# Three partial writes at the end of a kernel: waits between them removed, row numbers found on GpSimd

## The chip, the core and the metric

The kernel runs on one core of one Trainium2 chip. The metric is the time of one execution on the device, in microseconds (us). Within the core, TensorE (PE in the profile; PEld is its weight load) multiplies matrices, VectorE (DVE) and ScalarE (ACT) work elementwise, GpSimd (POOL) does small elementwise work and issues the indirect DMAs, and SyncE (SP) issues the other DMAs. A name with q (POOLq) is that engine's instruction sequencer.

## The reference

An attention block with normalized queries and keys, and behind it a mixture-of-depths block: of each batch's 448 tokens the 128 with the highest score go through two layers, and their rows of the output are replaced.

```python
# attention: batch 8, heads 12, seq 448, head_dim 64
q_n, k_n = rmsnorm(q, g_q), rmsnorm(k, g_k)
attn = softmax(scale * q_n @ k_n.T)           # over the keys
x = (attn @ v).transpose(0, 2, 1, 3).reshape(8, 448, 768)
# mixture of depths: D 768, F 1024, capacity 128
scores = np.einsum('bsd,d->bs', x, w_gate)
out = x.copy()
for b in range(B):
    top_idx = np.argpartition(-scores[b], capacity)[:capacity]
    xe = x[b, top_idx]
    h = np.maximum(xe @ w1, 0.0)
    ye = h @ w2
    g = 1.0 / (1.0 + np.exp(-scores[b, top_idx]))
    out[b, top_idx] = x[b, top_idx] + g[:, None] * ye
```

## The kernel before

`fast` holds the whole computation for the shapes at hand; `general` is compiled beside it, behind a branch (line 1436), and does not run here. The order of work is written out by hand: the loop at the end of `fast` goes through steps, in each of which it emits attention work, and one piece of the two layers' work of an earlier batch; `mixture` is a generator that is advanced one piece at a time.

Attention is tiled by groups of four heads. When a batch's attention is done, the whole batch x is stored to the output in DRAM (`store_x`, line 455, on SyncE's queue). Its scores are ranked, and `select` (line 539, GpSimd) writes the 128 selected rows by indirect DMA into a small DRAM buffer, from which they are loaded into `xe`, a tile of 128 partitions by 770 columns: 768 of the row, column `DM` (768) with the gate g, and column `DM + 1` with the row's number in the output.

`mixture` then computes the two layers for a group of batches. Batches 1 to 6 go in pairs; batch 0 and batch 7, the last, go alone. It transposes `xe` (line 610), finds the row numbers (line 622, VectorE), multiplies by w1 (line 639) and by w2 (line 659 or 683). `gated` (line 596, VectorE) multiplies a result in PSUM by the gate and adds it to `xe`; `write` (line 587, GpSimd) sends columns of `xe` by indirect DMA to those rows of the output that the tile `row` names.

For all batches but the last, one write sends whole rows of 768 columns. For the last, `parts_out` (line 583) cuts the columns into three parts, which are computed and written one after the other: columns 0 to 384, 512 to 768, and 384 to 512. Each write views the output as rows of the part's width, so each part needs its own row numbers: the number times 2, 3 or 6, plus 0, 2 or 3. `row` has one column for each part, and all three are computed by VectorE in one place, ahead of the layers.

The framework puts in the waits between engines and DMAs from the tiles and tensors that instructions read and write. All writes go to the tensor `out`, so each write of line 587 waits until the one before it has landed. `select` already lifts such waits for its four writes with `declare_no_dep`, as they go to different rows. In the build the last batch's second write waits for the first write's DMA and VectorE; the third waits for the second write's DMA, for an earlier DMA that used the same semaphore, and for VectorE.

Of the kernel before, what the change touches and what calls it, by code (L numbers as in the profile page):

```python
# [13 lines left out]
OP = mybir.AluOpType  # L14
# [54 lines left out]
def fast(  # L69
# [21 lines left out]
    nc = tc.nc  # L91
# [9 lines left out]
    DM = H * D  # L101
# [57 lines left out]
    for jj in range(NJ // 2):  # L159
# [4 lines left out]
        out=gg, in0=loads.gcol[:, 0:1], scalar=scale, in1=loads.gcol[:, 1:2], op0=OP.mult, op1=OP.mult  # L164
# [399 lines left out]
    def mixture(g):  # L564

        n, bs = CAP, groups[g]
        G = len(bs)
        wide = 128 * G
        xe = [xes.pop(b) for b in bs]
# [4 lines left out]
        def bank():  # L574

            if PER * now[0] >= units:
                return ps_sc.tile([128, 512], F32, tag="sc", name="sc")
            return ps_moe.tile([128, 512], F32, tag="moe", name="moe_ps")

        half = NDC // 2  # L580
        rows = []

        parts_out = ((0, HD), (DM - 2 * HD // 3, DM), (HD, DM - 2 * HD // 3)) if last else ((0, DM),)

        def write(i, k):
            c0, c1 = parts_out[k]
            nc.gpsimd.indirect_dma_start(  # L587
                out=out.flatten_outer_dims().rearrange("r (k c) -> (r k) c", c=c1 - c0),
                out_offset=bass.IndirectOffsetOnAxis(ap=rows[i][:n, k : k + 1], axis=0),
                in_=xe[i][:n, c0:c1],  # L590
                in_offset=None,
            )

        def gated(i, cols, ps):
            x = xe[i]
            nc.vector.scalar_tensor_tensor(  # L596
                out=x[:n, cols],
                in0=ps[:n, : cols.stop - cols.start],
                scalar=x[:n, DM : DM + 1],
                in1=x[:n, cols],  # L600
                op0=OP.mult,
                op1=OP.add,
            )

        for i, x in enumerate(xe):
            for a in range(2):
                ps = ps_sc.tile([128, 512], F32, tag="sc", name="xeT_ps") if a else bank()
                for d in range(half):
                    dc = half * a + d
                    nc.tensor.transpose(  # L610
                        out=ps[:, 128 * d : 128 * d + n],
                        in_=x[:n, 128 * dc : 128 * (dc + 1)],
                        identity=ident[:n, :n],
                    )
                nc.scalar.copy(  # L615
                    out=xeT[:, half * a : half * (a + 1), i, :n],
                    in_=ps[:, : half * 128].rearrange("p (i t) -> p i t", t=128)[:, :, :n],
                )
                if a == 1:
                    row = moe_pool.tile([128, len(parts_out)], I32, name="row", bufs=4)  # L620
                    for k, (c0, c1) in enumerate(parts_out):
                        nc.vector.tensor_scalar(
                            out=row[:n, k : k + 1],
                            in0=x[:n, DM + 1 : DM + 2],
                            scalar1=float(DM // (c1 - c0)),
                            scalar2=float(c0 // (c1 - c0)),
                            op0=OP.mult,
                            op1=OP.add,
                        )
                    rows.append(row)  # L630
                if a == 1 or G == 1:
                    yield

        chunks = 4 // G
        for f0 in range(0, NFC, chunks):
            ps = bank().rearrange("p (i g t) -> p i g t", g=G, t=128)
            for i in range(chunks):
                for dc in range(NDC):
                    nc.tensor.matmul(  # L639
                        out=ps[:, i, :, :n],  # L640
# [8 lines left out]
                out=hT[:, f0 : f0 + chunks, 0:G, :n], in_=ps[:, :, :, :n], func=AF.Relu  # L649
# [3 lines left out]
        if G == 1:  # L653
            for k, (c0, c1) in enumerate(parts_out if last else ((0, HD), (HD, DM))):
                ps = bank()
                h = c0 // HD
                for fc in range(NFC):
                    w = w2.get((fc // HF, h), ring.get("B12"))
                    nc.tensor.matmul(
                        out=ps[:n, : c1 - c0],  # L660
                        lhsT=hT[:, fc, 0, :n],
                        rhs=w[:, fc % HF, c0 - HD * h : c1 - HD * h],
                        start=(fc == 0),
                        stop=(fc == NFC - 1),
                    )
                    if fc == NFC // 2 - 1:
                        yield
                gated(0, slice(c0, c1), ps)
                if last or h:
                    write(0, k if last else 0)  # L670
                yield
            return
# [28 lines left out]
        for first in (0, 1) if PER * now[0] < units else (1, 0):  # L701
# [8 lines left out]
            if done_both:  # L710
                nc.vector.tensor_tensor(
                    out=s4[:, :, :n], in0=a12[:, :, :n], in1=s2[:, :, :n], op=OP.subtract
# [13 lines left out]
        product(ps, s4, w2[1, 1])  # L726
        gated(0, high, ps)
        write(0, 0)
        yield
        product(main, s3, ring[3], first=False)  # L730
# [7 lines left out]
        product(main, a22, ring[0], first=False)  # L738
        gated(1, low, main)
        write(1, 0)  # L740
        if g < len(groups) - 2:
            reload(1)
# [164 lines left out]
    def piece(q):  # L907

        nonlocal moe, done
        if half == 1 and single(q):  # L910
            return False
        pieces[0] += 1
        if next(moe, moe) is not moe:
            return True
        if ready.get(done, q + 1) > q:
            return False
        moe = mixture(done)
        pieces[:] = 1, 10 if len(groups[done]) == 1 else 17
        done += 1
        next(moe)  # L920
        return True
# [6 lines left out]
    while done < len(groups) or tasks:  # L928
        now[:] = q, 0
        k = PER * q  # L930
# [558 lines left out]
```

## Time and profile before

| | us |
|---|---|
| median of 3 runs | 518.45 (517.85 to 519.04) |
| the profiled execution | 513.42 |
| its span | 511.7 |
| PE busy in the span | 491.6 (96%) |
| DVE busy | 354.0 (69%) |
| ACT busy | 274.8 (54%) |
| POOL busy | 187.0 (37%) |

The profile is of one execution. The span runs from its first to its last instruction; what lies around it (1.7 us) belongs to the execution's time. Lines of the timeline give start, duration, engine, line, operation, tiles (out<-in), shapes, and in brackets the idle time before it on its engine and what ended that. A wait for several semaphores is put down to the one that came last.

### The profile page before, as it was taken

How to read it: one execution, taken by the hardware profiler on the slowest of the kernel's cores; microseconds unless marked ns; L12 is line 12 of the kernel's file. 1: busy time of each engine (PE TensorE's matmuls, PEld its weight loads, DVE VectorE, ACT ScalarE, POOL GpSimd, SP SyncE). 2: the span in 40 equal slices, each digit the busy share in tenths (PEclk: the TensorE clock that was granted, in tenths of full speed). 3: DMA queues.
4: the chain of work that ended last, by engine and by line, in shares of the span. 5: the costliest groups of instructions: out<-in, count | busy, mean ns of one | idle time of the engine just before them, and what ended most of it. 6: DMA issues, size and time to landing. Idle time of an engine off the chain costs nothing. (4 is left out here: it accounts for less than half of the span.)

```text
span 511.7 us, 11121 instructions
## 1 busy us (share of the span) xinstructions
PE 491.6 (96%) x4429; PEld 279.4 (55%) x4429; DVE 354.0 (69%) x670; ACT 274.8 (54%) x507; POOL 187.0 (37%) x104
## 2 busy tenths in 40 slices
PE   5999999988999999999999999999999899999994
PEld 4544445435555444666654454665554454786683
DVE  4566898699866898996687886777567686623201
ACT  4787886866757466665454737654634536310000
POOL 4694548444524174427123085036220022020102
PEclk9999999999999999999999999999999999999998
DMA  8977889999964673899461989567423318232601
GB/s 294 387 247 257 271 272 365 326 296 319 283 204 129 214 248 121 283 323 331 134 201 26 350 280 302 190 191 207 136 72 88 110 38 260 89 109 58 221 3 36
DMA packets 49295, 105.82 MB, mean 207 GB/s; under 512 B 11571, under 2 KB 26420, under 8 KB 49234
## 3 DMA queue, kind: packets, MB, share of 16 engines
q1 hardware_dynamic: 45826, 98.70, 59.9%
q0 software_dynamic: 3264, 6.31, 3.7%
q8 instruction: 37, 0.61, 0.5%
q14 instruction: 24, 0.20, 0.1%
q10 hardware_dynamic: 144, 0.00, 0.0%
HBM read 84.37 MB, written 28.50 MB: 221 GB/s over the span
## 5 line engine op out<-in xcount | busy, mean ns | idle before, releaser
L337 ACT ACTIVATE p<-sc,rinv 128x448 f32<-128x448 f32 x336 | 186.0, 641 | 88.3 <-PE sc L328 74.3
L256 POOL TENSOR_TENSOR rinv<-ss,neg_half 128x14 f32<-128x14 f32 (+1 forms) x49 | 135.7, 2775 | 184.4 <-DVE ss L255 164.9
L328 PE MATMUL sc<-qT,kT 64*64 64x448 f32 x1344 | 152.7, 545 | 1.0 <-DVE qT L307 0.8
L352 PE MATMUL av<-p,v 64*64 64x448 f32 x1344 | 147.0, 537 | 0.0
L368 DVE TENSOR_TENSOR sum<-sum,p 128x896 f32<-128x896 f32 x107 | 116.5, 1089 | 8.1 <-ACT p L337 1.9
L352 PEld LDWEIGHTS av<-p,v 64*64 64x64 f32 x1344 | 57.6, 133 | 69.6 <-issue 62.3
L328 PEld LDWEIGHTS sc<-qT,kT 64*64 64x64 f32 x1344 | 52.5, 132 | 69.3 <-issue 43.8
L255 DVE TENSOR_REDUCE ss<-sq 128x14 f32<-128x910 f32 (+1 forms) x49 | 52.1, 1074 | 11.9 <-ACT sq L246 11.6
L639 PE MATMUL moe_ps<-xeT,w 128*128 128x256 f32 (+1 forms) x288 | 56.1, 347 | 0.0
L539 POOL DMA_INDIRECT selected<-x,rank x32 | 35.8, 1118 | 47.7 <-DVE x L531 39.7
L639 PEld LDWEIGHTS moe_ps<-xeT,w 128*128 128x128 f32 x288 | 46.2, 191 | 6.8 <-issue 2.6
L246 ACT ACTIVATE sq<-tok 128x896 f32<-128x896 f32 (+1 forms) x49 | 45.9, 949 | 5.9 <-DMA tok<-in_tok_dram 5.6
L443 DVE TENSOR_TENSOR x<-x_ps,rden 112x512 f32<-112x512 f32 x48 | 32.5, 687 | 20.8 <-PE x_ps L441 18.3
L467 DVE SCALAR_TENSOR_TENSOR prod<-x,wg 112x256 f32<-112x256 f32 x96 | 40.6, 423 | 2.9
L587 POOL DMA_INDIRECT out_dram<-xe,row x10 | 10.5, 1052 | 85.7 <-DVE xe L596 67.9
L639 PE MATMUL sc<-xeT,w 128*128 128x256 f32 (+1 forms) x192 | 32.2, 328 | 0.3 <-ACT xeT L615 0.3
L441 PE MATMUL x_ps<-ident,xT 128*112 128x128 f32 x192 | 28.8, 276 | 2.0 <-DVE x L443 2.0
L639 PEld LDWEIGHTS sc<-xeT,w 128*128 128x128 f32 x192 | 28.8, 191 | 2.8 <-ACT xeT L615 0.5
L287 DVE SCALAR_TENSOR_TENSOR qT<-qT,gg,bc 128x896 f32<-128x896 f32 x22 | 25.3, 1149 | 4.4 <-DMA bc<-rows 4.4
L512 DVE SCALAR_TENSOR_TENSOR cmp<-score_rows,gate,earlier 112x448 f32<-112x448 f32 x32 | 21.9, 684 | 9.1 <-ACT score_rows L502 8.1
L441 PEld LDWEIGHTS x_ps<-ident,xT 128*112 128x112 f32 x192 | 21.8, 134 | 10.3 <-issue 4.5
L368 DVE TENSOR_TENSOR sum<-p 128x896 f32<-128x896 f32 x24 | 25.9, 1078 | 1.8 <-ACT p L337 1.8
(87 smaller groups left out, 331.9 us busy)
## 6 DMA issues: line engine op xcount, KB each, us to landing
tok<-in_tok_dram SPq DMA_DIRECT2D x48, 448.0 KB, 6.6
qT<-in_qT_dram SPq DMA_DIRECT2D x24, 448.0 KB, 6.6
kT<-in_kT_dram SPq DMA_DIRECT2D x24, 448.0 KB, 7.1
v<-in_vp_dram SPq DMA_DIRECT2D x24, 448.0 KB, 7.6
out_dram<-x SPq DMA_DIRECT2D x8, 1344.0 KB, 9.0
bc<-rows SPq DMA_DIRECT2D x44, 224.0 KB, 6.4
ring<-mixed SPq DMA_DIRECT2D x22, 384.0 KB, 5.3
xe<-selected SPq DMA_DIRECT2D x8, 385.0 KB, 3.7
```

The costliest lines, as they stand in the source:

```text
L246: nc.scalar.activation(out=sq[:, h, :, 0:D], in_=t[:, h], func=AF.Square, scale=scale)
L255: nc.vector.tensor_reduce(out=ss[:, h], in_=sq[:, h], axis=AX.X, op=OP.add)
L256: nc.gpsimd.tensor_tensor(out=rinv[:, h].rearrange(flat), in0=ss[:, h].rearrange(flat), in1=neg_half.to_broadcast([128, (h.stop - h.start) ...
L328: nc.tensor.matmul(out=scs[hh][D * c : D * (c + 1), 0:S], lhsT=get("kT", n)[r, c, D * i : D * (i + 1)], rhs=get("qT", n)[r, c, :], start=True,
L337: nc.scalar.activation(out=p[:, hh], in_=scs[hh][:, 0:S], func=AF.Exp, scale=rinvs[n, 1][:, hh, i : i + 1],)
L352: nc.tensor.matmul(out=avs[n][c][D * hh : D * (hh + 1), 0:S], lhsT=get("v", n)[r, hh, i, :], rhs=probs[u][r, hh], start=(i == 0), stop=(i ...
L368: nc.vector.tensor_tensor(out=sums[n], in0=probs.pop(u - 1) if begins else sums[n], in1=probs.pop(u), op=OP.add)
L441: nc.tensor.transpose(out=ps[:CP, j, :], in_=t[:, j, :], identity=ident)
L443: nc.vector.tensor_tensor(out=xs[b][:, :, col : col + 128].rearrange("p j (h d) -> p j h d", d=D), in0=ps[:CP].rearrange("p j (h d) -> p j ...
L467: nc.vector.scalar_tensor_tensor(out=prod[:, 0 : GH * D], in0=xs[b][:, j, cols], scalar=1.0, in1=wg[:, cols], op0=OP.mult, op1=OP.mult, ac ...
L539: w = nc.gpsimd.indirect_dma_start(out=t[:, :], out_offset=bass.IndirectOffsetOnAxis(ap=rank[:, j : j + 1], axis=0), in_=x[:, j, :], in_of ...
L639: nc.tensor.matmul(out=ps[:, i, :, :n], lhsT=w1[:, dc, 128 * (f0 + i) : 128 * (f0 + i + 1)], rhs=xeT[:, dc, 0:G, :n], start=(dc == 0), sto ...
```

## The change

`declare_no_dep` is called for the last batch's second and third writes, so that they do not wait for the writes before them in the same call of `mixture`. The row numbers of the first part (for the other batches the only part) are still found on VectorE, in the same place. Those of the second and third part are now found on GpSimd, each just ahead of its write.

```diff
         half = NDC // 2
-        rows = []
+        rows, written = [], []
...
+        def find_row(engine, i, k):
+            c0, c1 = parts_out[k]
+            engine.tensor_scalar(
+                out=rows[i][:n, k : k + 1],
+                in0=xe[i][:n, DM + 1 : DM + 2],
+                scalar1=float(DM // (c1 - c0)),
+                scalar2=float(c0 // (c1 - c0)),
+                op0=OP.mult,
+                op1=OP.add,
+            )
+
         def write(i, k):
             c0, c1 = parts_out[k]
-            nc.gpsimd.indirect_dma_start(
+            if k > 0:
+                find_row(nc.gpsimd, i, k)
+            w = nc.gpsimd.indirect_dma_start(
                 out=out.flatten_outer_dims().rearrange("r (k c) -> (r k) c", c=c1 - c0),
                 out_offset=bass.IndirectOffsetOnAxis(ap=rows[i][:n, k : k + 1], axis=0),
                 in_=xe[i][:n, c0:c1],
                 in_offset=None,
             )
+            for other in written if k > 0 else ():
+                tc.declare_no_dep(w.ins, other.ins, reason="other columns or other rows")
+            written.append(w)
...
                     row = moe_pool.tile([128, len(parts_out)], I32, name="row", bufs=4)
-                    for k, (c0, c1) in enumerate(parts_out):
-                        nc.vector.tensor_scalar(
-                            out=row[:n, k : k + 1],
-                            in0=x[:n, DM + 1 : DM + 2],
-                            scalar1=float(DM // (c1 - c0)),
-                            scalar2=float(c0 // (c1 - c0)),
-                            op0=OP.mult,
-                            op1=OP.add,
-                        )
                     rows.append(row)
+                    find_row(nc.vector, i, 0)
```

In the build the second write then waits for VectorE and for GpSimd's row number; the third for VectorE, for GpSimd's row number, and for the earlier DMA that used the same semaphore. The two row-number operations on GpSimd wait for nothing.

## The prediction

> **What bounds the kernel now.** I read the busy shares first, then the chain that ended last, then the timeline of the end, then the instructions and waits of line 587. Over the whole span TensorE is the bound:
>
> ```profile
> PE 491.6 (96%) x4429; PEld 279.4 (55%) x4429; DVE 354.0 (69%) x670; ACT 274.8 (54%) x507; POOL 187.0 (37%) x104
> ```
>
> Nothing on TensorE changes, so the question is the piece of the span in which TensorE is done. The chain that ended last shows it:
>
> ```profile
> 5 pieces in order of time: start us, us, what
> 504.15 0.96 DMA out_dram<-xe,row
> 505.11 2.63 issue
> 507.74 0.04 POOLq L1436
> 507.77 0.19 issue
> 507.96 0.96 POOL out_dram L587
> ```
>
> The third write starts at 507.96, 2.85 us after the second was issued, with nothing but that write's journey in between. The timeline has the three writes (L587) and the three vector operations that make their data (L596):
>
> ```profile
> 499.19 0.62 DVE L596 SCALAR_TENSOR_TENSOR xe<-sc,xe 128x384 f32<-128x384 f32 x1 [16.29 <-PE sc L659]
> 500.51 0.95 POOL L587 DMA_INDIRECT out_dram<-xe,row  x1 [16.55 <-DVE xe L596]
> 502.64 0.48 DVE L596 SCALAR_TENSOR_TENSOR xe<-sc,xe 128x256 f32<-128x256 f32 x1 [2.84 <-PE sc L659]
> 504.15 0.96 POOL L587 DMA_INDIRECT out_dram<-xe,row  x1 [2.69 <-issue]
> 504.43 0.35 DVE L596 SCALAR_TENSOR_TENSOR xe<-sc,xe 128x128 f32<-128x128 f32 x1 [1.30 <-PE sc L659]
> 507.96 0.96 POOL L587 DMA_INDIRECT out_dram<-xe,row  x1 [2.85 <-issue]
> ```
>
> Data are ready at 499.81, 503.12 and 504.78; writes begin 0.70, 1.03 and 3.18 us later. Line 587 between 500.6 and 504.2 shows what the GpSimd sequencer waited for (columns: count, min/median/max ns, first and last start):
>
> ```profile
> L587 POOL DMA_INDIRECT out_dram<-xe,row x2: 954/956/958, 500.5 to 504.1; - x2
> L587 POOLq EVENT_SEMAPHORE  x2: 17/1650/3282, 503.1 to 503.9; - x2
> DMA to landing us min/median/max: 2.6/2.8/3.0
> ```
>
> The first semaphore wait, that of the second write on the first, is over at 503.1: 500.51 plus the 2.6 us landing. The second, that of the third on the second, lasts 3.28 us, from 503.9 to 507.2: 504.15 plus 3.0. So the two waits are of quite different worth: the second write's data come at 503.12, just as the first write lands; the third write's data wait 2.4 us for a landing.
>
> At the end SyncE waits for all writes, then the engines meet and stop:
>
> ```profile
> SPq L1413 <- DMA out_dram<-xe,row: 24.2, 1, 24.2
> L1413 POOLq DRAIN  x3: 45/113/2559, 508.2 to 511.4; - x3
> L1413 DVEq DRAIN  x2: 10/26/41, 507.6 to 511.2; - x2
> ```
>
> The third write lands 2.3 us after its start, at about 510.3, and the closing takes 1.4 us to 511.7. VectorE reaches its closing DRAIN only at 507.6, PE at 505.7: these would matter if the third write landed before 507.6.
>
> **What the change leaves alone.** The built instruction lists of PE, ACT and SP are the same instruction for instruction; so is GpSimd's up to the first of these writes. Batches before the last have one part and one row-number operation, still on VectorE. The change therefore acts after 482.6 us only.
>
> **Removed: two VectorE operations** (row numbers 2 and 3; three such operations of 142 ns ran from 482.6). VectorE is idle from there to 499.19, waiting for TensorE: worth 0. That idle stretch is the cover; without it they would be worth 0.28 us at most.
>
> **Removed: the second write's wait for the first.** It ended at 503.1, the data at 503.12. Worth between 0 and, if the late wait is why that start came 1.03 instead of 0.70 us after the data, 0.33 us. I take 0, as the write now waits for two things again (VectorE and GpSimd's own row number): start 504.15, end 505.11.
>
> **Added: row number 2 on GpSimd**, issued behind the first write. GpSimd is idle from 501.46 to 504.15 and the operation waits for nothing, so it is ready before the data at 503.12 if it takes under 1.6 us. No row shows this operation on GpSimd. The nearest are small operations with an int32 side, and above them the power:
>
> ```profile
> L196 POOL CAST token_f<-token_i 112x4 f32<-112x4 int32 x1 | 0.2, 186 | 0.1
> L195 POOL IOTA token_i<- 112x4 int32 x1 | 0.1, 127 | 0.0
> L256 POOL TENSOR_TENSOR rinv<-ss,neg_half 128x7 f32<-128x7 f32 x2 | 3.0, 1491 | 1.7 <-DVE ss L255 1.7
> ```
>
> One value per partition, multiply and add: between 0.13 (IOTA) and 1.5 us (seven powers). I take 0.2, by the cast, since that is a plain conversion like this. Cost here 0.
>
> **Added: row number 3 on GpSimd**, queued behind the second write. It starts about 0.1 us after 505.11 and ends at 505.4. This one is not covered: the third write waits for it, and only for it, since the data (504.78) are older.
>
> **Removed: the third write's wait for the second.** In the build it now waits for VectorE, for GpSimd's row number, and for the earlier user of its semaphore, a write of selected rows from 454.58 that landed long ago. From the release to a write's start the trace has two prices: 0.27 us where the write stood ready (data at 476.59 and 482.72, writes at 476.86 and 483.00), and 0.78 where a semaphore wait went just before (507.18 to 507.96). Row number 3 at 505.4 gives 505.7 or 506.2. I take the middle, 505.9, since one wait (on data, 504.78) will be over early and the other not.
>
> **The sum.** The third write moves from 507.96 to 505.9: −2.06 us. It issues for 0.96 as before, lands 2.3 us after its start, at 508.2, behind VectorE's DRAIN at 507.6, so the closing still hangs on the write. Contention: the second write's 128 KB move within 505.6 to 506.8 in the trace, the third's 64 KB from about 507.4; no overlap. Span 511.7 − 2.06 = 509.64. The profiled execution took 513.42 (1.72 around its span) and would take 511.36. The median of the runs is 518.45, 5.03 above the profiled one; I carry that over: 518.45 − 2.06 = 516.4.
>
> Bounds: everything good, the second write 0.27 after its data (503.4, ends 504.35), row number 3 done at 504.65, third write 0.27 after its data: 505.05, −2.9. Everything poor, the second write 0.3 later for its extra wait, row number 0.4, start 0.78 behind that: 506.7, −1.25.
>
> **Two rules against the change.** *Row*: on GpSimd the first IOTA and the first CAST of the program follow each other at 37.99 and 38.18 with no gap, and the first two powers average 1491 ns: no cold start. *Rule*: the Trainium skill, GPSIMD Engine Reference, § 2.1, says the first call of a freshly loaded library kernel pays about 6 us for its code, which no profiled instruction shows. By the rule row number 2 would end at 507.6, the third write would start at 509.4 and the span end at 513.1: +1.4, 519.9. By the row, −2.06. [...]
>
> **Rivals.**
> *A new wait takes the old one's place.* Row number 3 stands between the two writes on GpSimd. If it costs what the power does, 1.49 us, the third write starts at 505.11 + 0.1 + 1.49 + 0.78 = 507.5: −0.5, 518.0, no change that can be told. For: software operations on GpSimd are dear here (2.8 us for 14 powers). Against: the cast.
> *Slower: cold code.* The 6 us above, paid once, at row number 2. Place: GpSimd after 501.46. Up to about 1.9 us it is hidden by the wait for data; from there it delays both writes, and beyond 1.9 + 2.06 = 4 us the kernel is slower than before: 519.9 at 6. Against: no first use in this trace shows it.
> *It does not do what it says.* If something else held the third write behind the second, say room for descriptors, nothing would be won: 518.4. Against: at 454.58, 455.82, 457.07 and 458.32 four such writes of 128 rows leave 1.25 us apart though each takes 2.4 to 3.0 us to land.
>
> **How the numbers follow.** Two kernels can be told apart here from 0.2% on, 1.04 us. The main course has 0.82 (gain 1.25 to 2.9, 515.5 to 517.2); the new wait or something holding the write 0.10 (517.5 to 518.5); cold code 0.05; an unseen loss in the closing 0.03 (about 518). Run-to-run spread is ±0.6 on the median. Of the main course nearly all is faster by over 0.2%, and a little of the second rival: faster 0.84, same 0.10, slower 0.06. The range takes the bounds and part of the spread: 515.2 to 517.7.
>
> **What would show it.** Right: the long semaphore wait of line 587 (3.28 us) gone; two small GpSimd operations, near 501.6 and 505.2, of about 0.2 us; the third write near 505.9; the second still near 504.15; GpSimd's issue to landing unchanged. Wrong: a third write after 507, a row-number operation over 1 us or a gap before it, a second write later than 504.5, or a closing over 1.4 us after the last landing.

## The result and the profile after

| | before | after |
|---|---|---|
| median, all runs side by side | 517.89 us (22 runs, 513.88 to 520.69) | 516.17 us (22 runs, 513.47 to 520.07) |
| ratio, 95% interval | | 0.9988 (0.9965 to 1.0011) |
| a second session, e1 below | 515.32 us (23 runs) | 514.76 us (12 runs), ratio 0.9991 (0.9961 to 1.0021) |
| profiled execution, span | 513.42, 511.7 us | 513.47, 511.8 us |

The medians moved by 1.7 and 0.6 us the way that was forecast (the ratio of the first two medians alone is 0.9967), but both intervals include no change at all. The runs of one kernel lie 5 to 7 us apart, several times what is looked for. They follow TensorE's granted clock: of the 22 runs of after, the one at 513.47 had 1.000 and the one at 520.07 had 0.991.

The profile has to decide, and its two spans are equal too. The timeline of after (GpSimd's writes are now L600, the gate additions L612) shows why:

```profile
501.05 0.62 DVE L612 SCALAR_TENSOR_TENSOR xe<-sc,xe 128x384 f32<-128x384 f32 x1 [16.41 <-PE sc L667]
502.37 0.95 POOL L600 DMA_INDIRECT out_dram<-xe,row  x1 [16.55 <-DVE xe L612]
503.34 0.21 POOL L587 TENSOR_SCALAR row<-xe 128x1 int32<-128x1 f32 x1
504.50 0.48 DVE L612 SCALAR_TENSOR_TENSOR xe<-sc,xe 128x256 f32<-128x256 f32 x1 [2.84 <-PE sc L667]
505.80 0.99 POOL L600 DMA_INDIRECT out_dram<-xe,row  x1 [2.24 <-DVE xe L612]
506.28 0.35 DVE L612 SCALAR_TENSOR_TENSOR xe<-sc,xe 128x128 f32<-128x128 f32 x1 [1.30 <-PE sc L667]
506.87 0.18 POOL L587 TENSOR_SCALAR row<-xe 128x1 int32<-128x1 f32 x1
507.41 1.00 POOL L600 DMA_INDIRECT out_dram<-xe,row  x1 [0.36 <-POOL row L587]
```

In this execution the first gate addition starts at 501.05, in that of before at 499.19. That is 1.86 us of drift in work that the change doesn't touch: in a second profile of the changed kernel (e1) it starts at 499.37. So times at the end are counted from that operation on, and its distance to the end of the span is called the tail. It is 12.52 us before (511.71 − 499.19) and 10.70 after (511.75 − 501.05). The third write starts at 8.77 before and at 6.36 after.

Two views confirm what released it. In the chain of after, the end of it, the long "issue" of before is gone; the data, the row number and the write follow each other:

```profile
506.28 0.36 DVE xe L612
506.65 0.03 POOLq L600
506.68 0.11 POOL out_dram L600
506.79 0.08 issue
506.87 0.18 POOL row L587
507.05 0.14 issue
507.18 0.04 POOLq L1444
507.22 0.18 issue
507.41 1.00 POOL out_dram L600
```

And the sequencer's semaphore waits for line 600 from 500 us on: the wait of 3282 ns is gone, the longest is 1043 ns, until the third part's data are there:

```profile
L600 POOLq EVENT_SEMAPHORE  x2: 17/530/1043, 505.0 to 505.6; - x2
```

### The profile page after: what moved, and what is told of

It reads as the page before. It is cut to its first block, busy times and chain, and to the rows that moved or that the text cites. A ratio compares the mean times of both kernels' runs of the same rounds, so it can differ in the third digit from the quotient of the medians.

```text
span 511.8 us, 11121 instructions
## 1 busy us (share of the span) xinstructions
PE 493.3 (96%) x4429; PEld 280.1 (55%) x4429; DVE 354.0 (69%) x668; ACT 274.8 (54%) x507; POOL 188.1 (37%) x106
## 4 chain that ended last, share of the span: by engine, by line
PE 60%; ACT 1%; DVE 1%; issue 0%; POOL 0%; POOLq 0%; ACTq 0%
PE sc L328 13%; PE av L352 13%; PE moe_ps L647 8%; PE moe_ps L691 6%; PE sc L647 6%; PE side_ps L691 5%; PE x_ps L441 2%; PE sc L667 2%; PE den_ps L396 1%; ACT p L337 1%; PE denT_ps L420 1%; PE moe_ps L667 1%; PE row_ps L496 0%; DVE xe L612 0%; PE xeT_ps L626 0%
## 5 line engine op out<-in xcount | busy, mean ns | idle before, releaser
L600 POOL DMA_INDIRECT out_dram<-xe,row x10 | 10.7, 1066 | 82.9 <-DVE xe L612 70.1
```

## The experiments

Starts and tails are in us after the first gate addition. "Landing" is from the third write's start to the moment SyncE saw it landed. Each row is one profile of its kernel; before and after have two.

| | second write | third write | landing | tail |
|---|---|---|---|---|
| before / e12 before again | 4.96 / 4.97 | 8.77 / 8.48 | 2.35 / 2.31 | 12.52 / 12.20 |
| after / e1 after again | 4.75 / 4.74 | 6.36 / 6.37 | 2.96 / 3.19 | 10.70 / 10.95 |
| e2 waits only | 4.22 | 5.87 | 3.46 | 10.73 |
| e3 third only | 4.73 | 6.37 | 2.98 | 10.74 |
| e4 rows only | 4.73 | 8.57 | 2.31 | 12.27 |
| e5 late third | 4.75 | 7.09 | 3.27 | 11.75 |
| e6 swap, before | 4.66 | 7.81 | 2.26 | 11.48 |
| e7 swap, after | 4.74 | 6.36 | 2.31 | 10.09 |
| e8 swap, waits only | 4.22 | 5.87 | 2.27 | 9.55 |
| e11 no third write | 4.75 | – | – | 9.46 |

**e1, the changed kernel again.**

> The changed kernel again, for its time beside the kernel before on one chip. The tail is counted from the start of the first of the three vector operations that add the gate (384 columns) to the end of the span: 12.52 us in the profile of before (511.71 - 499.19), 10.70 in that of after (511.75 - 501.05). Theory (the third write no longer waits for the second's landing, and the rest of the span is untouched): tail 10.3 to 10.9, third write 6.3 to 6.5 after the first vector operation (8.77 before), time 1.5 to 2.2 us shorter, ratio about 0.996 to 0.997. Rival (the gain is eaten elsewhere): same tail, but ratio 1.000 or above.

Tail 10.95, span 510.3; ratio 0.9991 (0.9961 to 1.0021). The tail agrees with the theory, nearly, and repeats. The ratio stays between the two: the expected 0.996 to 0.997 lies inside the interval, and so does 1.000.

**e12, the kernel before again**, for the spread on the other side.

> The kernel before once more, for the spread of its tail, which so far rests on one profile (12.52) and on the kernel with the row numbers moved and the waits kept (12.27). Theory (the tail of before is set by two landings one after the other): 12.1 to 12.8, the third write's wait 2.9 to 3.4 us long. Rival (12.52 was a long one, and the gain of 1.6 to 1.8 us is partly chance): 11.8 or less.

Tail 12.20, the wait 2.99 us. With two profiles on each side the gain in the tail is 12.36 − 10.83 = 1.5 us (1.25 to 1.8 by pairs).

**e2, waits lifted, row numbers left on VectorE.** A memset of a tile that nobody reads stands where the row numbers stood, so that there still is a GpSimd instruction ahead of each write.

```diff
             if k > 0:
-                find_row(nc.gpsimd, i, k)
+                nc.gpsimd.memset(moe_pool.tile([128, 1], F32, name="spacer", bufs=2), 0.0)
...
-                    find_row(nc.vector, i, 0)
+                    for k in range(len(parts_out)):
+                        find_row(nc.vector, i, k)
```

> The waits are lifted, but all three row numbers are found on VectorE as in the kernel before; ahead of the second and third write a 128x1 memset on GpSimd, of a tile that nobody reads, stands between the writes in place of the row numbers. Theory (lifting the wait is all; the row numbers on GpSimd only add a wait on GpSimd itself): second write 4.2 to 4.75 after the first vector operation (after: 4.75), third 5.6 to 6.2 (after: 6.36), tail 10.0 to 10.7, so equal to the changed kernel or up to 0.7 better. Rival (it is the row numbers on GpSimd that help, VectorE's signal being slow): tail 11.5 to 12.5.

The timeline of e2:

```profile
502.51 0.48 DVE L612 SCALAR_TENSOR_TENSOR xe<-sc,xe 128x256 f32<-128x256 f32 x1 [2.84 <-PE sc L668]
503.27 0.96 POOL L600 DMA_INDIRECT out_dram<-xe,row  x1 [1.82 <-DVE xe L612]
504.24 0.11 POOL L599 MEMSET spacer<- 128x1 f32 x1
504.30 0.35 DVE L612 SCALAR_TENSOR_TENSOR xe<-sc,xe 128x128 f32<-128x128 f32 x1 [1.30 <-PE sc L668]
504.93 0.96 POOL L600 DMA_INDIRECT out_dram<-xe,row  x1 [0.58 <-DVE xe L612]
```

With one thing to wait for, both writes start 0.28 us after their data (502.99 and 504.65), 0.5 us earlier than in after. So the rival falls: the row numbers on GpSimd don't help. In after the second write starts 0.8 us after its data, behind a separate semaphore wait; the third is then late because the second is still issuing, to 506.79, and its row number follows that. Yet the tail is 10.73, no better, and just over the expected range. The landing took 3.46 us instead of 2.3. Something else holds the end; e5 to e8 look for it. As a whole e2 has the lowest ratio here, 0.9968 (0.9935 to 1.0001), but not clearly faster than before or after.

**e3, only the third write freed; e4, only the row numbers moved.**

```diff
-            for other in written if k > 0 else ():
+            for other in written if k > 1 else ():    # e3
+            for other in ():                          # e4
```

> As the changed kernel, but only the third write's waits are lifted; the second still waits for the first to land. Theory (the second write's wait ended as its data came, and is worth 0 to 0.3): second write 4.7 to 5.1 after the first vector operation, third 6.3 to 6.8, tail 10.7 to 11.0. Rival (both waits carry the gain, as they stand in one chain): tail 11.5 or more.

> The row numbers of the second and third part on GpSimd, all waits between the writes kept. Theory: the writes start as before, 4.9 to 5.2 and 8.7 to 9.1 after the first vector operation; tail 12.4 to 12.9; the row numbers take about 0.2 us each and stand ready before their data or landings. Rival (the row numbers' place is what helps): tail under 12.

e3's tail is after's (10.74), and so is its third write's start; e4's tail is before's (12.27, a little under the expected 12.4, and its two writes start 0.1 to 0.2 us earlier than expected). The whole gain is the third write's wait; the second's was worth nothing that shows beside a row number on GpSimd. In both, the second write starts at 4.73 instead of 4.96, so these 0.23 us don't come from the lifted wait. They need no row number either: in e6 below, which has none on GpSimd, it starts at 4.66. Where they come from is open.

**e5, the third write later**, by finding its row number three times.

```diff
-                find_row(nc.gpsimd, i, k)
+                for _ in range(3 if k == 2 else 1):
+                    find_row(nc.gpsimd, i, k)
```

> The changed kernel with the third part's row number found three times over on GpSimd, so that the third write starts some 0.5 us later. What is tested: in the changed kernel and in the one with the waits lifted alone the third write starts 6.36 and 5.87 after the first vector operation, yet both tails are 10.7; in both, one of the third write's packets starts only when the 16 KB of instructions that are fetched from 6.9 to 8.3 after the first vector operation have passed. Theory (the fetch, not the write's start, now sets the end): third write at 6.8 to 7.0, tail 10.6 to 11.0. Rival (the tail follows the write's start, one for one, and the kernel with the waits alone was an accident): tail 11.2 to 11.5.

The write started at 7.09 and the tail was 11.75: neither. The end is no fixed floor, as the theory had it: 0.73 us later start, 0.8 to 1.05 us longer tail. The landing was again 3.27 us, with another fetch in the way (below). So the theory was formed anew: not one fetch at a fixed time, but any instruction fetch that overlaps the write's data delays a share of them.

The DMA view of after from 507.9 to 509.9, in slices of 0.05 us, and of 509.35 to 509.9 in slices of 0.014 us, shows the coincidence. First the long window:

```profile
GB/s 0 0 82 0 0 0 328 0 0 0 0 0 0 164 0 0 0 0 0 0 0 492 246 328 164 0 0 0 0 0 82 0 0 0 0 0 0 0 0 0
q8 instruction: 1, 0.02, 3.8%
```

then the short one:

```profile
GB/s 0 0 0 0 0 298 0 0 0 0 0 0 0 0 0 0 0 0 0 0 0 0 0 0 0 0 0 0 0 0 0 0 0 0 0 0 0 0 0 0
q0 software_dynamic: 2, 0.00, 4.9%
```

The value 328 at 508.2 is the 16 KB instruction packet; 3.8% of 16 engines over 2 us is 1.22 us, so it ends at 509.42. Of the third write's 16 packets of 4 KB, 15 start from 508.98 to 509.14. The last one starts at 509.42, in the short window, just as the fetch ends. The trace has such a straggler in each of the five profiles, counted again from the first gate addition: 8.37 (fetch ends 8.38) in after, 8.49 (8.50) in e1, 8.27 (8.28) in e2, 8.32 (8.32) in e3; in e5 it is 9.38, and the fetch that ends at 9.39 is a later one of 8 KB. In e2 the other 15 start from 7.40 to 7.55, so its earlier start gained nothing.

**e6 to e8, no jump at the end.** The general code is placed ahead of the fast code, so that the engines jump at the start, and not over the general code at the end.

```diff
-        with tc.If(is_small > 0) as cmp, tc.manual_schedule():
+        with tc.If(is_small < 1) as cmp:
+            general(tc, *(ap[n] for n in _INS), cap, out)
+        with cmp.Else(), tc.manual_schedule():
             fast(
                 tc, loads, *(ap[n] for n in _INS[5:]), cap, out,
             )
-        with cmp.Else():
-            general(tc, *(ap[n] for n in _INS), cap, out)
```

> The kernel before, with the two branches of the program in the other order: the general code first, the fast code last, so that the jump over the general code falls at the start and not at the end. Theory: no 16 KB instruction fetch by VectorE near the end, tail 12.0 to 12.6, since here the third write came after the fetch anyway; the start is up to 3 us longer for the jump. Rival (the fetch comes with the end of the program, wherever the code lies): a 16 KB fetch as before at 7.2 after the first vector operation.

> The changed kernel with the two branches in the other order. Theory (the instruction fetch holds one share of the third write): without the fetch the third write lands 2.3 to 2.5 after its start as in before, not 2.95, tail 10.0 to 10.4. Rival (the landing is slow because the second write's data are still under way): tail 10.7 to 10.9 as with the fetch.

> Waits lifted alone (row numbers on VectorE, a memset between the writes), with the two branches in the other order. Theory: the third write's earlier start now counts, tail 0.4 to 0.5 shorter than that of the changed kernel in the same order, 9.5 to 9.9. Rival (something else in the closing holds the end): equal to it within 0.15. For the whole: the jump at the start costs up to 3 us, so the time may be longer than that of the changed kernel.

The trace has no instruction fetch behind the first gate addition in any of the three. In e7, line 600 from 513 us on:

```profile
L600 POOL DMA_INDIRECT out_dram<-xe,row x1: 998/998/998, 513.2 to 513.2; - x1
DMA to landing us min/median/max: 2.3/2.3/2.3
```

The write starts at 6.36 as in after, lands in 2.3 us, and the tail is 10.09 instead of 10.70 to 10.95. In e8 the earlier start of the waits-only kernel now counts: 9.55, 0.54 less. Both are as expected, and the rivals fall. The second write's data were not in the way: in after its last packet has passed at 7.24, and the third write's first starts at 7.93. The closing is the same: 1.4 us from the third write's landing to the end of the span, in after as in e7. e6 shows that the kernel before paid too, which its expectation had missed: its second write landed in 2.43 us instead of 3.07 (2.78 in e12), and the tail is 11.48, under the expected 12.0. In before an 8 KB fetch runs from 6.56 to 6.88, and the second write's last two packets start at 6.88 and 7.22. So with no fetch in the way the change is worth 11.48 − 10.09 = 1.4 us, and lifting the waits alone 1.9.

The order is no remedy: the other order costs far more at the start than the expected 3 us. The 500th matmul starts at 51.7 to 54.8 in e6 to e8, and at 45.6 to 46.4 in the kernels with three or two parts and the old order; ratios 1.0122 (1.0058 to 1.0185) for e7 and 1.0130 (1.0055 to 1.0204) for e8.

**e9 and e10, six parts,** to bring the wait into the whole time.

```diff
-        parts_out = ((0, HD), (DM - 2 * HD // 3, DM), (HD, DM - 2 * HD // 3)) if last else ((0, DM),)
+        parts_out = tuple((128 * k, 128 * (k + 1)) for k in range(6)) if last else ((0, DM),)
...
-            for other in written if k > 0 else ():
+            for other in ():                          # e9 only
```

> The last batch in six parts of 128 columns instead of three, row numbers on GpSimd as in the changed kernel, all waits between the writes kept. It makes the disputed wait large enough for the whole time to show it. Theory (each write waits for the one before to land): writes 3.4 to 3.8 us apart, five such steps, end of the span 21 to 23.5 us after the first of six vector operations, time 6 to 8 us over the kernel before, ratio 1.012 to 1.016. Rival (landings overlap, the wait is not in the way): under 1.005.

> The same six parts, with the waits lifted as in the changed kernel. Theory: writes follow their data, 1.6 to 1.9 us apart, the last one 9.8 to 10.6 after the first vector operation, end 14 to 15; whole time 0.993 to 1.000 of the kernel before, 8 to 9 us (1.6%) shorter than with the waits. Rival (what the waits free is lost in issue on GpSimd, now with a row number in front of each write): writes over 2.2 us apart, less than 6 us gained.

The last writes of e9, and then of e10:

```profile
508.54 1.00 POOL L600 DMA_INDIRECT out_dram<-xe,row  x1 [2.60 <-DMA out_dram<-xe,row]
512.23 1.00 POOL L600 DMA_INDIRECT out_dram<-xe,row  x1 [2.44 <-DMA out_dram<-xe,row]
515.35 1.00 POOL L600 DMA_INDIRECT out_dram<-xe,row  x1 [1.86 <-DMA out_dram<-xe,row]
```

```profile
507.50 1.00 POOL L600 DMA_INDIRECT out_dram<-xe,row  x1 [0.53 <-POOL row L587]
509.29 1.00 POOL L600 DMA_INDIRECT out_dram<-xe,row  x1 [0.53 <-POOL row L587]
511.07 1.00 POOL L600 DMA_INDIRECT out_dram<-xe,row  x1 [0.53 <-POOL row L587]
```

Released by a landing the writes come 3.1 to 3.9 us apart, released by their data 1.7 to 1.9. The tails are 21.85 and 15.39, a difference of 6.5 us. The whole time shows it: 1.0105 (1.0066 to 1.0144) against 0.9996 (0.9960 to 1.0031), or 5.6 us of 517 (4.0 by the medians). The first ratio is a little under the expected 1.012, and the gain is less than the 8 to 9 us expected, as e9's steps were short (3.4 us on average) and e10's last write met a fetch again (3.7 us to land; tail 15.39, expected 14 to 15). That it is under 6 us is what the rival said, but not for its reason, as the writes are not over 2.2 us apart. So what the tail gains, the whole gets, as far as these runs can tell. e10 has three such stragglers, at 8.96, 10.58 and 12.71, beside fetches that end at 8.97, 10.58 and 12.73.

**e11, no third write.** The last 128 columns of the selected rows are not written.

```diff
-                if last or h:
+                if (last and k < 2) or (h and not last):
```

> The changed kernel without the third write (128 columns of the last batch's selected rows stay as they were stored before): what is left at the end when this write costs nothing. Theory (the second write's landing at 7.8 and VectorE's arrival at 8.2 after the first vector operation are next): tail 9.0 to 9.4, so that 1.3 to 1.7 us of the changed kernel's tail are still the third write's. Rival (the closing, with its instruction fetches, sets the end by itself): tail 10.4 or more.

Tail 9.46, just over the expected range: of after's tail 1.2 to 1.5 us are still the third write's, and no more is to be had from it. The second write now lands last, at 8.1, again 1.4 us before the end.

## Why the prediction was right or wrong

- **The time.** Forecast 516.4; measured 516.17, but beside 517.89 for the kernel before. That the two agree to 0.2 us is partly luck: the median of before came out 0.56 lower than the one the forecast was set on, and single runs lie up to 7 us apart. The forecast ratio, 0.9960, lies just below both intervals (0.9965 and 0.9961), so the forecast gain was somewhat too large; the 0.9971 that the tails give lies within both. "Faster by over 0.2%" at 0.84 was too sure: the interval includes no change, and 0.2% was not what the measurement could tell; with 22 runs a side it was 0.23% either way. Three close runs of before had made the spread look like ±0.6 us; it was ±3.
- **Work before 482.6 us untouched**: right as far as the runs show; the two profiles differ there by drift, as e1's first gate addition (499.37) is back beside before's (499.19).
- **VectorE's two operations worth 0**: right, e4's tail is before's.
- **The second write's wait worth 0**: right (e3), and for the reason given: the write waits for two things again. With the row numbers left on VectorE, in e2, it starts at 4.22. The start in after was not 504.15 − 499.19 = 4.96 but 4.75.
- **Row numbers on GpSimd at 0.2 us**: right, 0.21 and 0.18 us. *Cold code* falls by the same rows: the first of its kind took 0.03 us more than the second. What the Trainium skill, GPSIMD Engine Reference, § 2.1, tells of the first call of a freshly loaded kernel, 6 us, did not show. (The working of that rival has two slips: 509.4 takes the low price of 0.27 us for both starts, where the main course took the middle; and the time that row number 2 may take unnoticed is 1.6 us in one place and 1.9 us in the other.) *Something else holds the third write* falls with the third write at 6.36. *A new wait in the old one's place*, at 1.49 us, falls too; what the moved row numbers cost in all is the 0.5 us by which e2's third write starts earlier.
- **The third write's start**: forecast 505.9, which is 6.71 on this count; measured 6.36. Mis-sized by 0.35, because the second write was 0.21 earlier and the start came 0.36 behind the row number's end, not 0.5.
- **The step that failed: "lands 2.3 us after its start" and "Contention: no overlap".** It landed after 2.96 and 3.19 us, so the sign "GpSimd's issue to landing unchanged" did not come true. I had looked only at the second write's data. The instruction fetch behind VectorE's jump I had counted only as a late DRAIN of VectorE's; it is in the way of DMA packets too, and the write had been moved under it. The trace of before had it in sight, in the DMA view from 505 to 507:

  ```profile
  q8 instruction: 1, 0.02, 4.2%
  ```

  That is one packet of 1.34 us (4.2% of 16 engines over 2 us), from 506.43 to 507.77, across the 507.4 at which the freed write's data were to start. In before itself the third write's data came after it, at 509.5. This took 0.6 to 0.9 us of the 2.1 to 2.4 by which the start moved, and left 1.5 of the 2.06 forecast.
- **Still open**: the gain in whole time is not resolved by itself; both ratios are compatible with the tail's 1.5 us and with nothing.

## What to carry to other kernels

When a wait on a landing is lifted, ask not only when the write can start, but what will be moving on the DMA engines when it does: here the freed write slid under an instruction fetch and gave back a quarter to two fifths. In e2, where each freed write waits for its data alone, it starts 0.28 us after them; in after, with a separate wait ahead of it, the second write starts 0.8 us after them. So let the instruction ahead of a write be one that the write needs nothing from. (This is no general price: the first write waits for its data alone too, and starts 0.70 us after them in every profile here; why is open.) And where runs spread by 1%, count the changed stretch from an event just ahead of it, and enlarge the effect once (six parts) to see that the whole time follows.

## What the runs showed of the hardware

The jump over the general code at the end is followed by instruction fetches, and these were in the way of data. VectorE's jump in after starts at 506.3, and its closing DRAIN only at 509.2; in e7, without the jump, it drains at once, at 512.1, when its last operation starts:

```profile
L1421 DVEq DRAIN  x2: 10/25/40, 509.2 to 511.2; - x2
```

```profile
L1421 DVEq DRAIN  x2: 19/205/391, 512.1 to 516.4; - x2
```

The Trainium skill, Runtime: NRT & Kernel Launch, § Instruction fetch mechanics, says that a taken jump out of the window of fetched code forces a fetch before execution goes on. The traces agree (2.9 us from jump to DRAIN) and add the price for others: a packet of a data write waited until a 16 KB fetch of 1.2 to 1.4 us had passed.

Two things here are inferred from times. The first is that the 16 KB fetch is VectorE's. The traces name no engine for it, but it starts 1.7 to 2.1 us after VectorE's jump in every profile with up to three parts and the old order, in before too, where GpSimd jumps only after the fetch has begun; in e9 and e10 VectorE jumps 3.7 us later, and a 16 KB fetch starts 2.3 and 2.8 us after that. For which part of the fetch VectorE's DRAIN waits is open, as in after it comes 0.27 us before the packet ends. The second is that the fetch and the late packet share one of the 16 DMA engines: each straggler of the third writes is one of 16 packets, the other 15 are not late, and it starts within 0.02 us of the end of a fetch.
